# Two layers of cached-attention decode: one record of each round loaded in five pieces by rows, where it was one load of 128 rows

## The chip, the cores and the metric

The kernel runs on one core of a Trainium2 chip. The metric is the device time of one execution in microseconds. Before the change it is 730.65 us, the median of three runs (729.78 to 731.41).

## The reference, cut to what matters

A decode step for a batch of 4, one new position each, width 640. Two blocks are applied twice, with the same weights and the same cache both times: sliding-block attention over the last 1024 cached positions of 32 heads, and an MLP with a relu.

```python
x = A_x                                              # (4, 1, 640)
for _ in range(2):
    x = x + attention(layernorm(x))
    x = x + mlp(layernorm(x))

def attention(x):                                    # 32 heads of 128, no sharing of heads
    q = heads(x @ wq)                                # wq (640, 4096)
    k = k_cache[:, :, Sk - W:, :]                    # (4, 32, 1024, 128), W = 1024
    v = v_cache[:, :, Sk - W:, :]
    p = softmax(einsum("bhqd,bhkd->bhqk", q, k) * 128 ** -0.5)
    return join(einsum("bhqk,bhkd->bhqd", p, v)) @ wo   # wo (4096, 640)

def mlp(x):
    return maximum(x @ w1, 0) @ w2                   # w1 (640, 1728), w2 (1728, 640)
```

All of it is float32. The keys and values of one head for four batch rows are 4 MB, so over 32 heads and two rounds some 300 MB come from HBM.

## The kernel before, in words

**Records.** The host packs, for each head, everything that its attention needs into one record: an array of 128 rows and `REC` = 9472 columns (line 41), with the head's part of `wq`, the keys, the values and its part of `wo` side by side (`WQ`, `K`, `V`, `WO`, line 40). A row of a record is 37,888 bytes, lies in one partition, and is contiguous in HBM.

**Rounds.** A round is one attention block and one MLP. Round 0 goes through heads 0 to 31. Round 1 starts with the last five heads, 27 to 31, whose records are still in SBUF from round 0, and then takes heads 0 to 26 (`order`, line 126). So round 1 loads 27 records where round 0 loads 32.

**Buffers.** Five slots hold one record each (`NS`, line 45, and `slot`, line 108), and a ring of `RING` columns holds `w1` and `w2` in round 0 and takes the first records of round 1. `home` (line 129) says which slot a head's record goes to.

**The list of loads.** The kernel writes out all loads in order before it computes anything: `items` is a list, `load` (line 138) appends to it, `piece` (line 141) appends a range of columns of one record, `ending` (line 144) cuts the last three records of a round into seven column pieces (and, in round 0, three more for `wo`). Lines 154 to 165 write round 0's list: the first record in two pieces, then one load of all columns for each head of `hs[1:-3]`, the ending, five loads of `w1`, six of `w2`. Lines 168 to 189 write round 1's: ten loads that bring two records into the ring and freed slots, eight half records, one load of all columns for each head of `new[6:-3]`, the ending, four loads of `w1`, four of `w2`. That is 51 loads in each round.

**Issue.** `pump` (line 191) issues loads from the head of that list on SP's queue as long as the columns that they fill aren't live; each entry becomes one `dma_start` over all 128 partitions (line 197). `done` (line 212) frees columns when their last reader has been written out, and calls `pump`. Waits on semaphores are put in by the framework: SP waits for the readers of what a load overwrites, and TensorE waits for the loads whose columns it reads. `InOrder` (line 63) keeps the instructions of TensorE, VectorE, ScalarE and SP each in the order in which the program writes them; through it every instruction carries line 77 in the profile.

**The work on one record** (lines 373 to 394): `query` multiplies the normalized input with the record's part of `wq`, `query_T` transposes the result, `scores` makes 16 matmuls over the keys, `exponentials` runs on ScalarE, `weights_T` transposes the weights, `values` makes 64 matmuls over the values, `output_T` and `project` add the head's share to an accumulator in PSUM. The query of the next record is written ahead of the values of this one. After the last record of a round come `center` and `mlp`. The `busy` matmuls (line 229) between them write to a place that nothing reads.

All matmuls of a record read all 128 partitions of the columns concerned.

Of the kernel before, what the change touches and what calls it, by code (L numbers as in the profile page):

```python
# [31 lines left out]
P = 128  # L32
# [8 lines left out]
REC = 2 * D + 8 * W  # L41
# [13 lines left out]
W1_SLOT = [[0, 1], [2], [3], [4]]  # L55
W2_SLOT = [22, 20, 8, 4]
LATE = 3


IDENT, MEAN, NCON = 0, 128, 256  # L60
# [24 lines left out]
def decode_kernel(ctx: ExitStack, tc: tile.TileContext, xf, cst, rec, w1, w2, out):  # L85
    nc = tc.nc
    pe, dve, act, sp = (InOrder(tc, e) for e in (nc.tensor, nc.vector, nc.scalar, nc.sync))
# [12 lines left out]
    on = sb.tile([P, DH], F32, name="on")  # L100
    oTs = sb.tile([P, LATE, B], F32, name="oTs")
    qs = sb.tile([P, DH], F32, name="qs")
# [26 lines left out]
    def home(h, r):  # L129

        return h % NS if not r or h >= LAST else (h - 6 + LAST) % NS

    items = []
    at = {}
    live = []
    buffers = dict(enumerate(slot)) | {"ring": ring}

    def load(key, src, lo, hi, buf, col):
        items.append((key, src, lo, hi, buf, col))

    def piece(r, h, lo, hi, buf=None, col=None):
        load(("rec", r, h), rec[h], lo, hi, home(h, r) if buf is None else buf, lo if col is None else col)

    def ending(r, hs, late):
        a, b, c = hs[-3:]
        end = WO if late else REC
        for h, lo, hi in ((a, 0, V), (b, 0, V), (a, V, end), (c, 0, V), (b, V, end), (c, V, V + VH), (c, V + VH, end)):
            piece(r, h, lo, hi)
        if late:
            for h in hs[-3:]:  # L150
                piece(r, h, WO, REC)


    hs = order[0]
    piece(0, hs[0], 0, V)
    piece(0, hs[0], V, REC)
    for h in hs[1:-3]:
        piece(0, h, 0, REC)
    ending(0, hs, True)
    for k, col in enumerate(W1_RING):  # L160
        load(("w1", 0), w1, k * FF, k * FF + FF, "ring", col)
    n = 0
    for size, col in W2_RING:
        load(("w2", 0), w2, n * FD, (n + size) * FD, "ring", col)
        n += size


    hs = order[1]
# [10 lines left out]
        piece(1, new[i], 0, V, *((old[i], 0) if i < 5 else ("ring", 0)))  # L179
        piece(1, new[i], V, REC, old[i - 1], V)  # L180
    for h in new[6:-3]:
        piece(1, h, 0, REC)
    ending(1, hs, False)
    for blocks in W1_SLOT:
        load(("w1", 1), w1, blocks[0] * FF, (blocks[-1] + 1) * FF, home(LAST + 1, 0), blocks[0] * FF)
# [5 lines left out]
    def pump():  # L191

        while items:
            key, src, lo, hi, buf, col = items[0]
            if any(b == buf and x < col + hi - lo and col < y for b, x, y in live):
                return
            sp.dma_start(buffers[buf][:, col:col + hi - lo], src[:, lo:hi])
            live.append((buf, col, col + hi - lo))
            at.setdefault(key, []).append((lo, hi, buf, col))
            items.pop(0)  # L200
# [11 lines left out]
    def done(key, lo, hi):  # L212

        if key[0] == "rec" and key[1] == 0 and key[2] >= LAST:
            return
        for x, y, buf, col in pieces(key):
            a, b = col + max(lo, x) - x, col + min(hi, y) - x
            if a < b:
                rest = []
                for bb, u, v in live:  # L220
                    if bb != buf or v <= a or b <= u:
                        rest.append((bb, u, v))
                    else:
                        rest += [(bb, p, q) for p, q in ((u, a), (b, v)) if p < q]
                live[:] = rest
        pump()
# [6 lines left out]
    def center(fill):  # L233

        x = acc[:, :FD]
        dve.tensor_reduce(sums, x, op=OP.add, axis=AX.X)
        if fill:
            busy(256)
        pe.matmul(misc[:, 0:1], mean_of, sums, start=True, stop=True)
        if fill:  # L240
            busy(512)
            busy(256)
        dve.tensor_scalar(xc, x, misc[:, 0:1], None, op0=OP.subtract)
        dve.transpose(xT, xc)
        act.activation(square, xc, AF.Square, accum_out=squares)
        dve.tensor_copy(x_sb, x)
# [113 lines left out]


    pump()
    residual()
    for r in range(2):
        hs = order[r]
        late = LATE if r == 0 else 1
        center(r > 0)
# [78 lines left out]
```

## Time and profile before

| | before |
|---|---|
| median of 3 runs | 730.65 us (729.78 to 731.41) |
| the profiled execution, own time | 731.21 us |
| its span, first to last instruction | 729.4 us |
| mean granted TensorE clock | 0.854 |
| HBM read | 304.04 MB, 417 GB/s over the span |

How to read what follows. The page names engines PE (TensorE's matmuls), PEld (its weight loads), DVE (VectorE), ACT (ScalarE), POOL and SP; SPq is SP's DMA queue. Shares are of the span. In the strip of 40 slices a digit is a busy share in tenths, and "DMA" is the mean over the core's 16 DMA engines. A group line gives engine, operation, tiles, count, busy time and mean length of one, and behind the bar the idle time of that engine just before, with what ended it. An issue line gives count, size and the median time from issue to landing. A line of the chain of waits gives start, length and what it was. A row of the table by stretches gives the stretch, its length, busy time and count for PE, PEld, DVE, ACT and POOL, the granted clock, the DMA engines' mean share, and GB/s.

### The profile page before, as it was taken

Reading aid. Unit: us, or ns where it says so; the run is one execution under the profiler, and the core shown is the slowest. Engines: PE = TensorE matmul, PEld = TensorE weight load, DVE = VectorE, ACT = ScalarE, POOL = GpSimd, SP = SyncE. Lnnn points to the kernel's source line nnn. Section 1 sums busy time; section 2 is a strip of 40 time slices with the busy share of each in tenths; the row PEclk is TensorE's granted clock in tenths of the full one; section 3 lists DMA queues with packets and bytes.
Section 4 is the critical chain, followed back from the end, with each engine's and each line's share of the span. In section 5 each row is a group of like instructions: output and inputs, shape, how many; then the busy total and the mean of one; then the engine's idle time right before and its main releaser. Section 6 shows DMA issues by size and latency. Waiting matters only on the chain.

```text
span 729.4 us, 15682 instructions
## 1 busy us (share of the span) xinstructions
PE 517.4 (71%) x7300; PEld 266.3 (37%) x7300; DVE 179.2 (25%) x541; ACT 90.3 (12%) x154; POOL 0.2 (0%) x4
## 2 busy tenths in 40 slices
PE   0766867568667485778789888675857766667876
PEld 0233433334334243334433555332433333333532
DVE  1212222122222122212312334212212222122420
ACT  0201011011010101101111111101101011010110
POOL 0000000000000000000000000000000000000000
PEclk9978787787788777878999999968878888787999
DMA  9999999999999999999999999999999999999994
GB/s 377 432 430 431 428 431 431 430 431 431 430 431 431 430 431 430 431 431 411 417 375 376 408 427 423 433 429 430 431 431 432 429 431 428 431 430 420 424 421 199
DMA packets 15185, 305.12 MB, mean 418 GB/s; under 512 B 1681, under 2 KB 2065, under 8 KB 5137
## 3 DMA queue, kind: packets, MB, share of 16 engines
q1 hardware_dynamic: 14832, 303.91, 98.0%
q8 instruction: 57, 0.93, 0.5%
q10 hardware_dynamic: 288, 0.21, 0.1%
q14 instruction: 8, 0.06, 0.0%
HBM read 304.04 MB, written 0.08 MB: 417 GB/s over the span
## 4 chain that ended last, share of the span: by engine, by line
DMA 76%; PE 20%; DVE 2%; issue 1%; ACT 0%; SPq 0%; DVEq 0%; ACTq 0%
DMA slot<-rec 71%; PE sc_ps L77 7%; PE o_ps L77 4%; PE pt_ps L77 4%; DMA slot<-w 3%; DMA ring<-w 2%; PE q_ps L77 2%; PE acc L77 2%; PE misc L77 2%; DVE on L77 1%; DVE small L77 1%; DVE oTs L77 0%; ACT prob L77 0%; DVE qs L77 0%; SPq L77 0%
## 5 line engine op out<-in xcount | busy, mean ns | idle before, releaser
L77 PE MATMUL sc_ps<-slot,qT 128*1 128x512 f32 x992 | 152.8, 745 | 1.6 <-DVE qT L77 0.9
L77 PE MATMUL q_ps<-slot,xT 128*4 128x128 f32 x620 | 49.8, 333 | 133.1 <-DMA slot<-rec 132.3
L77 ACT ACTIVATE prob<-sc_ps,small 128x1024 f32<-128x1024 f32 x64 | 71.3, 1114 | 566.0 <-DVE small L77 557.2
L77 PE MATMUL o_ps<-slot,pT 128*1 128x128 f32 x4056 | 122.4, 273 | 5.2 <-DMA slot<-rec 4.3
L77 PEld LDWEIGHTS o_ps<-slot,pT 128*1 128x1 f32 x4056 | 99.3, 84 | 63.5 <-issue 46.8
L77 DVE TENSOR_REDUCE small<-sc_ps 128x1 f32<-128x1024 f32 x64 | 78.3, 1224 | 149.6 <-PE sc_ps L77 149.6
L77 PE MATMUL pt_ps<-con,prob 128*128 128x128 f32 x518 | 113.2, 360 | 0.0
L77 PEld LDWEIGHTS pt_ps<-con,prob 128*128 128x128 f32 x518 | 81.8, 185 | 23.2 <-issue 22.2
L77 PEld LDWEIGHTS q_ps<-slot,xT 128*4 128x4 f32 x620 | 21.4, 89 | 155.5 <-DMA slot<-rec 148.6
L77 DVE TENSOR_SCALAR qs<-q_ps,small 128x128 f32<-128x128 f32 x64 | 22.4, 350 | 209.9 <-PE q_ps L77 209.7
L77 PEld LDWEIGHTS sc_ps<-slot,qT 128*1 128x1 f32 x992 | 21.6, 92 | 82.0 <-issue 76.4
L77 PE MATMUL misc<-con,on 128*128 128x128 f32 x64 | 21.0, 328 | 30.5 <-DVE on L77 30.5
L77 PE MATMUL acc<-slot,oTs 128*4 128x160 f32 x512 | 29.1, 299 | 15.7 <-DVE oTs L77 15.5
L77 DVE COPY pT<-pt_ps 128x16 f32<-128x16 f32 x128 | 22.1, 174 | 62.5 <-PE pt_ps L77 62.5
L77 DVE TENSOR_SCALAR on<-o_ps,small 128x128 f32<-128x128 f32 x64 | 22.4, 350 | 35.0 <-PE o_ps L77 35.0
L77 PEld LDWEIGHTS misc<-con,on 128*128 128x128 f32 x64 | 8.9, 139 | 49.3 <-DVE on L77 49.3
L77 PE MATMUL misc<-con,qs 128*128 128x128 f32 x64 | 24.6, 385 | 2.3 <-DVE qs L77 2.1
L77 PE MATMUL sc_ps<-slot,con 128*1 128x512 f32 (+1 forms) x50 | 20.8, 506 | 0.0
L77 PEld LDWEIGHTS acc<-slot,oTs 128*4 128x4 f32 x512 | 7.2, 84 | 27.8 <-DVE oTs L77 27.7
L77 DVE COPY oTs<-misc 128x4 f32<-128x4 f32 x64 | 10.4, 162 | 27.0 <-PE misc L77 27.0
L77 PEld LDWEIGHTS misc<-con,qs 128*128 128x128 f32 x64 | 12.0, 187 | 6.5 <-ACT small L77 2.2
L77 ACT ACTIVATION_READ_ACCUMULATOR prob<-sc_ps,small 128x1 f32 x64 | 12.3, 193 | 0.0
(45 smaller groups left out, 97.7 us busy)
## 6 DMA issues: line engine op xcount, KB each, us to landing
slot<-rec SPq DMA_DIRECT2D x46, 4736.0 KB, 36.6
slot<-rec SPq DMA_DIRECT2D x17, 2368.0 KB, 24.3
slot<-rec SPq DMA_DIRECT2D x5, 1024.0 KB, 34.6
ring<-w SPq DMA_DIRECT2D x5, 864.0 KB, 13.9
slot<-rec SPq DMA_DIRECT2D x2, 2048.0 KB, 43.3
slot<-rec SPq DMA_DIRECT2D x3, 1344.0 KB, 11.0
slot<-w SPq DMA_DIRECT2D x3, 864.0 KB, 32.7
ring<-rec SPq DMA_DIRECT2D x1, 2368.0 KB, 18.7
```

The lines of the kernel that those rows point to most:

```text
L77: r = build(*args, **kwargs)
```

## The change

`load` and `piece` get one more argument, a list of row ranges, which stands in each entry of `items`; `pump` issues one `dma_start` for each row range, all of the same columns. The list is `EVEN`, one range of all 128 rows, for every entry but two: the record of `hs[20]` in each round, head 20 in round 0 and head 15 in round 1 (`hs` is `order[1]` there), is loaded by the five ranges of `UNEVEN`, 96 rows and four times 8 rows. The same bytes go to the same places, in the same place of the list.

```diff
+EVEN = [(0, P)]
+UNEVEN = [(0, 96), (96, 104), (104, 112), (112, 120), (120, P)]
+SHIFTED = 20
...
-    def load(key, src, lo, hi, buf, col):
-        items.append((key, src, lo, hi, buf, col))
+    def load(key, src, lo, hi, buf, col, rows=EVEN):
+        items.append((key, src, lo, hi, buf, col, rows))
 
-    def piece(r, h, lo, hi, buf=None, col=None):
-        load(("rec", r, h), rec[h], lo, hi, home(h, r) if buf is None else buf, lo if col is None else col)
+    def piece(r, h, lo, hi, buf=None, col=None, rows=EVEN):
+        load(("rec", r, h), rec[h], lo, hi, home(h, r) if buf is None else buf, lo if col is None else col, rows)
...
     for h in hs[1:-3]:
-        piece(0, h, 0, REC)
+        piece(0, h, 0, REC, rows=UNEVEN if h == hs[SHIFTED] else EVEN)
...
     for h in new[6:-3]:
-        piece(1, h, 0, REC)
+        piece(1, h, 0, REC, rows=UNEVEN if h == hs[SHIFTED] else EVEN)
...
-            key, src, lo, hi, buf, col = items[0]
+            key, src, lo, hi, buf, col, rows = items[0]
...
-            sp.dma_start(buffers[buf][:, col:col + hi - lo], src[:, lo:hi])
+            for a, b in rows:
+                sp.dma_start(buffers[buf][a:b, col:col + hi - lo], src[a:b, lo:hi])
```

## The prediction, made before the changed kernel was run

> **What bounds the kernel now.** I read the page first (busy shares, the DMA strip, the chain that ended last), then the queue's own waits, the chain in order of time, and last the stretches at the end of each round in steps of 1 us.
>
> ```profile
> span 729.4 us, 15682 instructions
> PE 517.4 (71%) x7300; PEld 266.3 (37%) x7300; DVE 179.2 (25%) x541; ACT 90.3 (12%) x154; POOL 0.2 (0%) x4
> DMA  9999999999999999999999999999999999999994
> DMA packets 15185, 305.12 MB, mean 418 GB/s; under 512 B 1681, under 2 KB 2065, under 8 KB 5137
> q1 hardware_dynamic: 14832, 303.91, 98.0%
> q8 instruction: 57, 0.93, 0.5%
> DMA 76%; PE 20%; DVE 2%; issue 1%; ACT 0%; SPq 0%; DVEq 0%; ACTq 0%
> L77 PE MATMUL q_ps<-slot,xT 128*4 128x128 f32 x620 | 49.8, 333 | 133.1 <-DMA slot<-rec 132.3
> slot<-rec SPq DMA_DIRECT2D x46, 4736.0 KB, 36.6
> ```
>
> The loads bound it: SP's queue q1 keeps the 16 DMA engines moving 98% of the span, and TensorE's idle time is almost all before the query matmuls, 132.3 us of waiting for a record. A load lands 36.6 us after its issue, so some three loads always stand in line. The chain of waits gives the pace:
>
> ```profile
> 483.77 37.87 DMA slot<-rec
> 521.68 0.60 PE q_ps L77 x10
> ...
> 528.64 37.90 DMA slot<-rec
> 566.58 0.60 PE q_ps L77 x10
> ...
> 575.15 36.30 DMA slot<-rec
> ```
>
> Landings at 521.6 and 566.5 are 44.9 us and four records apart: 11.2 us a record. TensorE takes 575.15 - 566.58 = 8.6 us for one.
>
> The queue's packets tell how a load is split. The kernel's lists hold 51 loads for each round, and with the store of the result SP issues 103; 14832 / 103 = 144 = 128 + 16, and 103 x 16 = 1648 accounts for nearly all of the 1681 packets under 512 B. So a row of a load is one packet, moved whole by one engine, and each of the 16 engines closes its share with one small packet. In full stretches the DMA share is 1.00:
>
> ```profile
> 600.00:650.00 50.00, 33.31 (x455) 18.39 (x459) 11.60 (x36) 4.82 (x8) 0.00 (x0) 0.80 1.00 428
> 715.00:716.00 1.00, 0.93 (x9) 0.19 (x9) 0.00 (x0) 0.00 (x0) 0.00 (x0) 1.00 0.98 406
> 716.00:717.00 1.00, 0.92 (x6) 0.22 (x2) 0.00 (x0) 0.64 (x2) 0.00 (x0) 1.00 0.80 330
> 717.00:718.00 1.00, 1.00 (x6) 0.40 (x5) 0.17 (x1) 0.51 (x2) 0.00 (x0) 1.00 0.65 271
> 718.00:719.00 1.00, 0.14 (x2) 0.00 (x0) 0.21 (x1) 0.00 (x0) 0.00 (x0) 1.00 0.55 232
> 719.00:720.00 1.00, 0.43 (x16) 0.38 (x20) 0.00 (x0) 0.00 (x0) 0.00 (x0) 1.00 0.48 200
> 720.00:721.00 1.00, 1.00 (x38) 0.81 (x28) 0.00 (x0) 0.00 (x0) 0.00 (x0) 1.00 0.47 195
> 721.00:722.00 1.00, 0.37 (x8) 0.02 (x2) 0.00 (x0) 0.00 (x0) 0.00 (x0) 1.00 0.43 172
> 722.00:723.00 1.00, 0.00 (x0) 0.00 (x0) 0.00 (x0) 0.00 (x0) 0.00 (x0) 1.00 0.21 82
> 725.00:726.00 1.00, 0.93 (x20) 0.33 (x18) 0.00 (x0) 0.00 (x0) 0.00 (x0) 1.00 0.01 5
> ```
>
> The last two columns are DMA share and GB/s. They show the one thing on which this change can act: the engines don't finish together. The last loads are in every engine's line before 716, yet engines begin to stop at about 716.8, half of them have stopped by 719 (0.48 x 16 = 7.7 still move), and the last stops at 725.7. That is a slow half, up to 8.9 us behind the first engine, and a fast half, spread over 719.0 - 716.8 = 2.2 us. The instruction packets of q8 (57 of them, 0.93 MB, in the engines' lines beside the rows) are what can set engines apart; no row says which engines carry them. When others stop, an engine gets no faster (195 / 0.47 / 16 = 25.9 GB/s against 428 / 16 = 26.8), so the limit lies with each engine or with the rows that it writes, not with the memory. The same dip stands at the end of round one:
>
> ```profile
> 370.00:371.00 1.00, 0.97 (x12) 0.40 (x4) 0.32 (x1) 0.00 (x0) 0.00 (x0) 1.00 0.99 408
> 371.00:372.00 1.00, 1.00 (x5) 0.29 (x5) 0.77 (x3) 0.32 (x2) 0.00 (x0) 1.00 0.78 307
> 372.00:373.00 1.00, 1.00 (x11) 0.30 (x9) 0.17 (x1) 0.98 (x3) 0.00 (x0) 1.00 0.58 228
> 373.00:374.00 1.00, 1.00 (x7) 0.52 (x4) 0.00 (x0) 0.66 (x2) 0.00 (x0) 1.00 0.60 249
> ```
>
> Half the engines wait there too, for at least 3 us, so the slowest lags by 3 to 8.9 us; I take 6.
>
> **The change part by part.** *Removed:* one load of 128 rows in each round, 8 rows for each engine. A row is 4736 KB / 128 = 37,888 B; at 26.8 GB/s it takes 1.41 us, and 8 take 11.3, which agrees with the 11.2 us pace.
>
> *Added, the 96 rows:* 6 for each of 16 engines, 8.4 us.
>
> *Added, four loads of 8 rows:* as a row is one packet on one engine, such a load can use at most eight engines, so the eight that take part carry 6 + 4 = 10 rows of this record and the others 6. No load of fewer than 128 rows is in the trace, so one load's price is bounded from both sides. If only the engine limits, it is one row, 1.41 us. If the rows written limit, 8 rows get their 8/128 of 428 GB/s, 26.8 GB/s, and take 11.3 us. A price below 1.41 is excluded, since an engine gets no faster alone. The eight rows of one load are adjacent, and in the rows shown no eight rows ever receive more than one engine's rate; that leans away from the low end. But eight adjacent rows need not hang on one limit only, which leans away from the high one. I take the middle, 6.3 us. The eight engines then need 8.4 + 4 x 6.3 = 33.6 us for the record, 33.6 - 11.3 = 22.3 more than before (bounds 2.8 and 42.3).
>
> Here a rule of the Trainium skill bears on the price: SBUF — State Buffer, "Door 1: The DMA port swizzle", says that a transfer's rate follows how many of 16 ports its rows reach, about 27.2 GB/s a port, four adjacent rows on one port. By it eight rows reach two ports, and 303 KB take an estimated 5.6 us: 19.5 us more for the record instead of 22.3, and about 764 us in the end by the sum below. It speaks against the change; the rows above fit it as well as they fit a limit in the engine.
>
> *Where the delay goes.* The four small loads stand in line on the eight engines ahead of the next three records, so the record lands some 22 us late, TensorE starves there once, and its slot is released as late. The other engines don't run dry: they have the three records behind it, 33 us, in line. The eight engines never catch up inside a round (share 1.00), so every later record comes as late, at the old pace, up to the end of the round, where the last landing sets the MLP. Round two repeats it: its loads into the ring wait for TensorE to consume what lies there, so the first delay passes on whole.
>
> *The sum.* At the end of round two, if the eight are the fast half, the last landing moves from 725.7 to 719.0 + 22.3 = 741.3: +15.6. If they are the slow half: +22.3. In round one, with a fast half spread over 2 us and a lag of 6: +22.3 - 4 = +18.3, or +22.3. Together +33.9 or +44.6. No row tells which half takes the rows; I take the middle, +39.3.
>
> *Issues and waits:*
>
> ```profile
> L77 SPq DMA_DIRECT2D slot<-rec x76: 327/328/653, 1.2 to 667.3; - x76
> SPq L77 <- PE acc L77: 482.7, 53, 21.4
> SPq L77 <- DMA slot<-rec: 84.1, 21, 6.5
> ```
>
> Eight more issues of 328 ns are 2.6 us of SP, which already stands 482.7 us waiting for slots; they are hidden by the 36.6 us line of loads, and cost 1.3 us a round if that line were gone. SP also waits at times for an earlier load (up to 6.5 us); four more loads in flight can bring such waits for the next records' issues, with only later loads queued behind them, and 6.5 us is well inside the line. TensorE's first query matmul waits for five loads in place of one: nothing beside its present wait of some 3 us a record. I cost these at 0.
>
> The profiled execution took 731.21 us, 0.56 over the median of 730.65, and its span is 729.4. 731.21 + 39.3 = 770.5; against the median, 770 us.
>
> **The rivals.**
>
> *The engine alone limits, and the fast half takes the rows: faster.* A small load costs 1.41 us, the eight engines get 2.8 us more in each round and the others 2.8 less. In round two the slow half ends 8.9 - 2.8 = 6.1 us after the first stop and the fast half at 2.2 + 2.8 = 5.0: -2.8. In round one, 6 - 2.8 = 3.2 against 2 + 2.8 = 4.8, a gain of 1.2, or none if the fast half spreads over 3.2: I take -0.5. Sum -3.3, 727.3 us. For it: the two halves in the windows, and that two rows move just half the gap. Against it: it needs eight engines to write eight adjacent rows at 16 times the rate that eight rows get now over a whole load. It decides where a small load takes under (4 + 6.7 + 2 x 2.8) / 8 = 2.0 us; above that the loss outweighs. The Trainium skill has a rule for who takes them (DMA: Bandwidth & Descriptors, "Why a DMA increments its semaphore by 16 and not by 1"): eight rows run on the eight lowest-numbered engines. Nothing in the trace shows whether these are the fast ones.
>
> *The engine alone limits, and the slow half takes the rows.* +2.8 us in each round: 736.3 us. For it: the halves are as likely this way round.
>
> *The change does nothing to the engines' shares:* rows stay with the engine that writes them in a whole load, so each still moves 8. 730.7 us. For it: the limit may lie with the rows. Against it: a split by count gives 6 rows of 96 to each engine.
>
> **How the numbers follow.** Forecast (crowded rows) 0.55; faster rival 0.28; slow half at engine rate 0.08; nothing 0.09. The forecast's own range is 747 to 786: a small load of 4.1 us with the fast half gives 8.8 us less a round (+16.3, 747), one of 7.6 with the slow half 5.2 more (+55, 786). The high bound of 11.3 us would give over 800, which I hold at 0.05. To hold 8 in 10 the range reaches from the faster rival, 727, to 782; about 0.1 lies above. What this measurement can tell from no change is about 0.2%, 1.5 us. Faster: the second case and a little, 0.29. Same: most of the fourth, 0.08. Slower: the rest, 0.63.
>
> **What would show it.** The packets of q1: with eight engines on each small load the count rises by 2 x 32 to 14896 (four times eight more closing packets a round); with two engines each, by 16. The median landing of the 8-row loads and the wait of TensorE before the split record: near 25 us where the rows crowd, near 3 at engine rate. In the last stretches: a plateau of half the engines lasting some 20 us for the forecast; the first stop later and the last stop earlier for the faster rival. The forecast is wrong if the small loads take under 2 us each, or if the late engines catch up before the round ends.

## The result, and the profile after

The changed kernel takes 784.71 us (782.86 to 785.66, four runs) against 730.21 us for the kernel before in the same job: a ratio of 1.0744, 95% interval 1.0715 to 1.0773. It is 54.5 us slower. The forecast was slower, 770, with a range that ended at 782: the way was right, the size too small.

The page of the changed kernel, its heads and the strip of bandwidth:

```profile
span 782.9 us, 15696 instructions
DMA  9999999999999999999989999999999999999994
GB/s 383 433 432 431 431 431 432 433 424 429 428 355 171 225 431 431 431 428 419 409 327 360 420 428 434 430 429 429 431 431 225 125 376 433 431 431 419 427 420 197
q1 hardware_dynamic: 14896, 303.91, 97.7%
DMA 66%; PE 23%; another core or an unknown queue 8%; DVE 2%; issue 1%; SPq 0%; ACT 0%; DVEq 0%; ACTq 0%
L81 PE MATMUL q_ps<-slot,xT 128*4 128x128 f32 x620 | 51.5, 341 | 186.6 <-DMA slot<-rec 185.8
```

The loss stands in two places of the GB/s strip, slices 12 to 14 and 31 to 33, one in each round; elsewhere the rate is about what it was. The DMA share doesn't show it: the engines count as busy while a packet crawls. TensorE's wait for records rose from 132.3 to 185.8 us, by 53.5, which is the growth of the span (782.9 - 729.4). The 14896 packets are the number that the prediction gave for eight engines on each small load. The same matmul, the last projection of round 0, stands at these places of the chain of waits, in the changed kernel first and then in the kernel before:

```profile
397.46 0.46 PE acc L81 x8
```

```profile
369.88 0.45 PE acc L77 x8
```

So round 0 loses 27.6 us and round 1 the other 25.9 of the span's 53.5. The first place in steps of 4 us, in the changed kernel (the last two columns are DMA share and GB/s):

```profile
228.00:232.00 4.00, 1.30 (x29) 0.44 (x17) 0.72 (x4) 1.21 (x2) 0.00 (x0) 1.00 1.10 237
232.00:236.00 4.00, 1.12 (x11) 0.55 (x12) 0.07 (x1) 0.00 (x0) 0.00 (x0) 0.66 1.00 218
236.00:240.00 4.00, 4.00 (x21) 2.00 (x25) 0.81 (x4) 0.00 (x0) 0.00 (x0) 0.50 1.11 227
240.00:244.00 4.00, 3.26 (x81) 1.75 (x73) 1.81 (x4) 1.21 (x2) 0.00 (x0) 0.99 0.83 170
244.00:248.00 4.00, 0.15 (x7) 0.00 (x0) 0.00 (x0) 0.00 (x0) 0.00 (x0) 0.87 1.24 156
248.00:252.00 4.00, 0.00 (x0) 0.00 (x0) 0.00 (x0) 0.00 (x0) 0.00 (x0) 0.50 1.11 142
252.00:256.00 4.00, 0.00 (x0) 0.00 (x0) 0.00 (x0) 0.00 (x0) 0.00 (x0) 0.50 0.99 142
256.00:260.00 4.00, 0.00 (x0) 0.00 (x0) 0.00 (x0) 0.00 (x0) 0.00 (x0) 0.50 1.07 152
260.00:264.00 4.00, 0.00 (x0) 0.00 (x0) 0.00 (x0) 0.00 (x0) 0.00 (x0) 0.50 0.84 142
264.00:268.00 4.00, 0.00 (x0) 0.00 (x0) 0.00 (x0) 0.00 (x0) 0.00 (x0) 0.50 0.78 180
268.00:272.00 4.00, 0.00 (x0) 0.00 (x0) 0.00 (x0) 0.00 (x0) 0.00 (x0) 0.50 0.91 341
272.00:276.00 4.00, 3.78 (x23) 2.29 (x27) 0.88 (x4) 0.00 (x0) 0.00 (x0) 0.50 1.01 436
```

There are two steps. From 228 to 240 the rate is about half of 430, and from 244 to 264 it is a third, 142 to 156. Against 430 GB/s the eleven rows up to 272 lose 4 us x (430 - rate) / 430 each, 24.4 us together, most of the round's 27.6. The first figure behind the comma is TensorE's busy time: it has next to nothing to do from 244 to 272, since the split record is late. In the chain that wait has no name; it seems that the view doesn't recognize the completions of loads that fewer than 16 engines carry:

```profile
244.15 27.83 another core or an unknown queue
272.22 1.01 PE q_ps L81 x10
```

What ended it can be read from the completions in the trace, one for each engine that takes part in a load (16 for a load of 128 or 96 rows, eight for a small load). The first and the last completion of each load, in us:

| load | changed kernel, first and last | before, first and last |
|---|---|---|
| the record ahead, 128 rows | 227.99, 234.83 | 228.12, 231.55 |
| the split record: 96 rows (before: 128) | 244.98, 257.24 | 239.34, 242.78 |
| its four small loads, one after another | 250.08, 259.94; 254.19, 264.14; 258.90, 268.34; 262.88, 271.98 | |
| the record behind, 128 rows | 272.22, 282.95 | 250.57, 255.24 |

The last small load is complete at 271.98, where TensorE's wait ends. The prediction had that wait near 25 us if the rows crowd, and it is 27.8. The engine that is first has its part of the 96 rows at 244.98. Up to there no engine is on a small load, and the low rate is due to the 96 rows. Then the leading engines go on to the small loads while the last is on its 96 rows up to 257.24, so the second step mixes the two.

### The profile page after: what moved, and what is told of

Its sections match the earlier page's. It is cut to its first block, busy times and chain, and to the rows that moved or that the text cites. A ratio compares the mean times of both kernels' runs of the same rounds, so it can differ in the third digit from the quotient of the medians.

```text
span 782.9 us, 15696 instructions
## 1 busy us (share of the span) xinstructions
PE 518.4 (66%) x7300; PEld 269.8 (34%) x7300; DVE 179.2 (23%) x541; ACT 90.3 (12%) x154; POOL 0.2 (0%) x4
## 3 DMA queue, kind: packets, MB, share of 16 engines
q1 hardware_dynamic: 14896, 303.91, 97.7%
## 4 chain that ended last, share of the span: by engine, by line
DMA 66%; PE 23%; another core or an unknown queue 8%; DVE 2%; issue 1%; SPq 0%; ACT 0%; DVEq 0%; ACTq 0%
DMA slot<-rec 61%; PE sc_ps L81 7%; PE o_ps L81 5%; PE pt_ps L81 5%; DMA slot<-w 3%; PE q_ps L81 2%; DMA ring<-w 2%; PE acc L81 2%; PE misc L81 2%; DVE on L81 1%; DVE oTs L81 0%; DVE small L81 0%; SPq L81 0%; ACT prob L81 0%
## 5 line engine op out<-in xcount | busy, mean ns | idle before, releaser
L81 PE MATMUL q_ps<-slot,xT 128*4 128x128 f32 x620 | 51.5, 341 | 186.6 <-DMA slot<-rec 185.8
L81 PE MATMUL sc_ps<-slot,qT 128*1 128x512 f32 x992 | 150.0, 733 | 1.6 <-DVE qT L81 0.9
L81 PE MATMUL pt_ps<-con,prob 128*128 128x128 f32 x518 | 115.7, 367 | 0.0
L81 PEld LDWEIGHTS pt_ps<-con,prob 128*128 128x128 f32 x518 | 83.8, 189 | 24.1 <-issue 23.2
L81 PEld LDWEIGHTS acc<-slot,oTs 128*4 128x4 f32 x512 | 7.2, 84 | 27.8 <-DVE oTs L81 27.6
```

The source lines that it names most:

```text
L81: r = build(*args, **kwargs)
```

## The experiments

Fifteen kernels, each the changed kernel with the edit shown, unless said otherwise. Two kinds of theory ran through all of them: that adjacent rows crowd where they are written, in groups of partitions that share the rate of one engine (theory A), and that something else about the loads costs the time: their number (B), the unequal shares of the engines (C), or adjacent rows on the side that is read (D). The times are against the kernel before in the same job; one run each, except for `c5` (ten) and `shift` (five), so that differences of a microsecond or two between the others mean little. The changed kernel is +54.5. A comment behind a line of the edits names the kernel that has it.

| kernel | the split record of each round | difference, us |
|---|---|---|
| c5 | five loads by columns, all 128 rows | +0.9 |
| h64 | 2 x 64 adjacent rows | +33.1 |
| h32 | 4 x 32 adjacent rows | +32.5 |
| r96_32 | 96, then 32 adjacent rows | +31.6 |
| st32 | 4 x 32 rows, step 4 | +0.7 |
| h32_src | 4 x 32: partitions adjacent, HBM rows step 4 | +32.6 |
| st32_src | 4 x 32: partitions step 4, HBM rows adjacent | +0.2 |
| src_st | as changed, small loads read HBM rows with step 4 | +56.6 |
| st4 | 96, then 4 x 8 rows, step 4 | +42.6 |
| low | rows 32 on in one load of 96, then 4 x 8 adjacent of rows 0 to 31 | +42.2 |
| low_st | the same, small loads with step 4 | +32.3 |
| shift | 3 x 32 with step 4, 4 x 8 with step 4 | +14.5 |
| q23 | as changed, on the first 2,176 columns only | +11.1 |
| r0 | as changed, in round 0 only | +28.7 |
| probe | none; the very last load of `w2` as 112, 8 and 8 rows | +1.7 |

**The number of loads.** `c5` makes as many loads as the change, by columns.

```diff
+COLS = [(0, 1896), (1896, 3792), (3792, 5688), (5688, 7584), (7584, REC)]
...
-            for a, b in rows:
-                sp.dma_start(buffers[buf][a:b, col:col + hi - lo], src[a:b, lo:hi])
+            for a, b in cols or [(lo, hi)]:
+                sp.dma_start(buffers[buf][:, col + a - lo:col + b - lo], src[:, a:b])
```

> The record of hs[20] in five loads by columns, each over all 128 rows, in place of five loads by rows: as many loads, issues and semaphores as in the changed kernel. Theory A (rows crowd: a group of adjacent rows takes no more than one engine's rate, 27 GB/s, and only a load over all 128 rows keeps 16 engines out of each other's way): 0, within 1.5 us of before. Rival B (the number of loads, their issues and SP's waits for earlier loads cost the time): +20 to +54 us.

731.25 against 730.35 us, ratio 1.001 (1.0001 to 1.002). The number of loads, the issues and the waits of SP cost nothing that counts here.

**Equal shares for all engines.** `r96_32` and `h64` take the unequal shares away and leave the split by rows.

```diff
-UNEVEN = [(0, 96), (96, 104), (104, 112), (112, 120), (120, P)]
+UNEVEN = [(0, 96), (96, P)]       # r96_32
+UNEVEN = [(0, 64), (64, P)]       # h64
```

> 96 rows, then 32 rows in one load instead of four of 8: 6 and 2 rows for each of 16 engines, so no engine carries more than another. Theory A: the 96 rows take 17 us in place of 8.4 (2.8 us a row, as in the changed kernel's trace), the 32 rows, two engines to four adjacent rows, 5.6 in place of 2.8: +11 us a round, +22 in all. Rival C (only the eight engines with ten rows cost the time, each row at the engine's own rate or at a price of the small loads): 0 within 1.5 us.

> Two loads of 64 adjacent rows, 4 rows for each engine in each. Theory A in its stricter form (the groups that share a rate are four adjacent rows together with the four that lie 32 rows off, so 64 adjacent rows hold eight groups): each load at half rate, 11.3 us, +11.3 us a round, +22 in all, with two engines on each group throughout. If the groups are eight adjacent rows the same 64 rows hold eight groups too: +22. Rival C (the engines' shares alone count): 0 within 1.5 us.

+31.6 and +33.1. That unequal shares alone cost is out: here each engine moves eight rows of the record and more than half of the loss is still there. Both theories missed the size, A by a third: it has the two loads at half rate, which gives +22.

**Rows of a small load spread out.** `st4` takes the last 32 rows with a step of 4.

```diff
+UNEVEN = [(0, 96, 1), (96, P, 4), (97, P, 4), (98, P, 4), (99, P, 4)]
-                sp.dma_start(buffers[buf][a:b, col:col + hi - lo], src[a:b, lo:hi])
+                sp.dma_start(buffers[buf][a:b:n, col:col + hi - lo], src[a:b:n, lo:hi])
```

> The 96 rows as in the changed kernel, and the four loads of 8 rows taken with a step of 4 (rows 96, 100, ... 124, then 97, 101, ...), so that the eight rows of one load lie in eight groups of four. Same count of loads, same engines, same rows per engine. Theory A: each small load shares its groups only with the engines that write them anyway, 2.8 us in place of about 5: the record costs some 8 to 10 us less a round than in the changed kernel, so +54 falls to +30 to +40. Rival B or C (count of loads, or unequal shares of the engines at a fixed price): +54 as before.

+42.6, a little above what A said: 12 us of the loss are the adjacency inside the small loads. The completions agree: on the engine that is first a small load takes 3.1 us, where it takes 4.5 in the changed kernel. The 96 rows, which `r96_32` and `st4` share, take that engine 17.1 us in both.

**Read or written.** `src_st` leaves the partitions of the change as they are and spreads the rows that the small loads read; the host orders the last rows of two extra copies of the records.

```diff
+UNEVEN = [(0, 96, 0, 96, 1), (96, 104, 96, P, 4), (104, 112, 97, P, 4), (112, 120, 98, P, 4), (120, P, 99, P, 4)]
-                sp.dma_start(buffers[buf][a:b, col:col + hi - lo], src[a:b, lo:hi])
+                sp.dma_start(buffers[buf][a:b, col:col + hi - lo], src[c:d:n, lo:hi])
```

> As the changed kernel, the four small loads writing 8 adjacent partitions each, but reading from HBM rows that lie four rows apart (the host puts the last 32 rows of a copy of these two records in another order). Theory A (the rows written crowd): +54 as the changed kernel, within 2 us. Rival D (adjacent rows read from one place of HBM crowd): it falls to what the loads with step 4 on both sides gave, +42.6.

+56.6, 2 us above the changed kernel: no gain from reading elsewhere.

**The other end of the partitions.** `low` and `low_st` put the small loads on rows 0 to 31.

```diff
+UNEVEN = [(32, P), (0, 8), (8, 16), (16, 24), (24, 32)]                            # low
+UNEVEN = [(32, P, 1), (0, 32, 4), (1, 32, 4), (2, 32, 4), (3, 32, 4)]              # low_st
```

> The record as 96 rows from row 32 on, and rows 0 to 31 in four loads of 8 adjacent rows. If the small loads run on the eight engines that write rows 0 to 63 of a whole load (theory A with the lowest eight engines), four engines share a group of four rows while that group's own engine is one of the eight: 5.6 us a small load, four of them 22.5. Sum near the changed kernel: +45 to +58. Rival C: the same as the changed kernel, +54.

> The same with the rows 0 to 31 taken with a step of 4: the eight rows of a small load lie in eight groups, and if the small loads run on the eight engines that write those groups anyway, each row at most meets what the 96 rows left: 1.4 us a small load in place of 5.6. Theory A: 16.7 us a round less than with adjacent rows, some 33 us less in all, +15 to +28. If the small loads ran on the other eight engines, each group would be shared by two: 2.8 us, some 22 us less than with adjacent rows. Rival C (ten rows on eight engines at a fixed price): the same as with adjacent rows.

+42.2 and +32.3: both outside what A said, from opposite sides. The step helps here too, but by 10 us and not by 33. In `low_st` a row takes 2.9 us in the median between 228 and 250, while the 96 rows are under way, and 1.4 again from 254 on, as the last of them lands (254.9): most of its loss is that of the 96 rows. So A had the weights wrong: it put most of the loss into the small loads. Why small loads cost less on rows 0 to 31 than on 96 to 127, adjacent or not, is taken up under `shift`.

**Four loads of 32.** `h32` has them adjacent, `st32` with a step of 4.

```diff
+UNEVEN = [(0, 32), (32, 64), (64, 96), (96, P)]                                    # h32
+UNEVEN = [(0, P, 4), (1, P, 4), (2, P, 4), (3, P, 4)]                              # st32
```

> The record in four loads of 32 adjacent rows, two rows for each engine in each load. If a group that shares one engine's rate is four adjacent rows and the four that lie 32 rows off, 32 adjacent rows hold eight groups, two engines on each, half rate as with 64 adjacent rows: +33 as that kernel, within 8. If a group is eight adjacent rows, 32 rows hold four groups, quarter rate: 4 x 11.3 = 45 us a record in place of 11.3, +60 us or more in all. Rival C (only unequal shares of the engines cost): 0.

> The record in four loads of 32 rows taken with a step of 4, two rows for each engine in each load; each load's rows span all sixteen groups. If what counts is how many groups a load's rows reach: 0 to +3. If what counts is which groups the sixteen engines write at the same moment: engines e and e+4 of a half stand on one group in step, eight groups at a time: up to +33, less as far as the engines fall out of step.

+32.5 and +0.7. This is the sharpest pair: the same number of loads, of rows in a load, of rows for each engine, of bytes. While the split record loads, in `h32` first and then in `st32`:

```profile
228.00:232.00 4.00, 0.62 (x9) 0.11 (x8) 0.16 (x1) 0.22 (x2) 0.00 (x0) 0.85 0.94 208
236.00:240.00 4.00, 4.00 (x49) 2.34 (x51) 0.83 (x5) 0.00 (x0) 0.00 (x0) 0.79 0.96 208
248.00:252.00 4.00, 0.00 (x0) 0.00 (x0) 0.00 (x0) 0.00 (x0) 0.00 (x0) 0.50 0.85 180
256.00:260.00 4.00, 2.54 (x18) 1.99 (x19) 0.70 (x3) 0.00 (x0) 0.00 (x0) 0.50 0.90 369
```

```profile
228.00:232.00 4.00, 0.36 (x8) 0.24 (x9) 0.00 (x0) 0.00 (x0) 0.00 (x0) 0.61 0.97 417
236.00:240.00 4.00, 3.26 (x81) 1.85 (x77) 1.81 (x4) 1.21 (x2) 0.00 (x0) 1.00 1.06 449
244.00:248.00 4.00, 4.00 (x34) 2.40 (x37) 0.88 (x4) 0.00 (x0) 0.00 (x0) 0.75 1.01 436
```

About half the rate against the full rate. 32 adjacent rows are no slower than 64 (+32.5 and +33.1), which a group of eight adjacent rows would not allow. That engines which meet on one group would slow each other even with a step of 4 did not come about in `st32`.

**Which side, with the pair.** `h32_src` and `st32_src` take the two steps apart, with the host putting the rows of the two extra copies in the order that each needs.

```diff
+UNEVEN = [(slice(32 * j, 32 * j + 32), slice(j, P, 4)) for j in range(4)]          # h32_src: partitions, rows of HBM
+UNEVEN = [(slice(j, P, 4), slice(32 * j, 32 * j + 32)) for j in range(4)]          # st32_src
-                sp.dma_start(buffers[buf][a:b, col:col + hi - lo], src[a:b, lo:hi])
+                sp.dma_start(buffers[buf][to, col:col + hi - lo], src[of, lo:hi])
```

> Four loads of 32 adjacent partitions, each reading every fourth row of a copy of the record whose rows the host has put in the order that this needs. Theory A (the partitions written crowd): +32, as with 32 adjacent rows on both sides. Rival D (adjacent rows of HBM crowd): 0 to +2.

> Four loads to every fourth partition, each reading 32 adjacent rows of HBM. Theory A: 0 to +2, as with step 4 on both sides. Rival D: +32.

+32.6 and +0.2. The partitions that a load writes decide, the rows that it reads don't.

**By bytes, and by round.** `q23` splits 23% of the record's columns, `r0` splits in one round.

```diff
+            piece(0, h, 0, K + 1536, rows=UNEVEN)        # q23, and the same in round 1
+            piece(0, h, K + 1536, REC)
...
-        piece(1, h, 0, REC, rows=UNEVEN if h == hs[SHIFTED] else EVEN)
+        piece(1, h, 0, REC)                              # r0
```

> Only the first 2,176 of the record's 9,472 columns are loaded by 96 and four times 8 rows, the rest in one load of 128 rows; 23% of the bytes, and one load more than in the changed kernel. Theory A (each row that crowds costs its time): 0.23 x 54.5 = +12.5, within 4. Rival B (a price for each small load whatever its size): +54.

> The changed kernel with the split in round 0 alone. If the late engines never catch up inside a round and each round loses its own: half of +54, +26 to +29, and the end of round 1 as in the kernel before. If the loss of round 0 is partly made up in round 1: under +24.

+11.1, a fifth of 54.5 for 23% of the bytes: the price goes with bytes, not with loads. +28.7, half of it: each round loses its own, and nothing of it is made up later.

**Who carries the small loads.** `probe` is the kernel before, with its very last load cut so that the completions tell when the eight engines of a small load are through.

```diff
-        load(("w2", 1), w2, n * FD, (n + size) * FD, home(LAST + 2, 0), n * FD)
+        load(("w2", 1), w2, n * FD, (n + size) * FD, home(LAST + 2, 0), n * FD,
+             [(0, 112), (112, 120), (120, P)] if size == 4 else [(0, P)])
```

> The kernel before with nothing changed but its last load (w2, 2,560 bytes a row): 112 rows, then two loads of 8 rows, which show when the eight engines that small loads run on reach the end of their line. If these are the fast half: the two loads of 8 rows land 3 to 9 us before the load of 112 rows that stands ahead of them. If they are the slow half: after it. Time within 1.5 us of before.

The time is 1.7 us over before, a little more than was expected. The completions in the trace, one for each engine, in us:

```
112 rows   716.8 716.8 717.2 717.3 717.4 718.0 718.9 719.9   721.8 722.2 722.5 722.8 723.7 723.8 724.1 726.7
8 rows     717.0 717.0 717.5 717.5 718.2 720.0               722.1 723.9
8 rows     717.2 717.2 717.7 717.7 718.4 720.2               722.3 724.1
```

Six of the eight engines belong to the fast half and two to the slow one; the slowest, at 726.7, is not among them. Neither of the two expectations, all fast or all slow.

**The shift itself, with little to crowd.** `shift` gives ten rows to those eight engines and six to the others, as the change does, out of loads with a step of 4.

```diff
+UNEVEN = [(0, P, 4), (1, P, 4), (2, P, 4), (3, 32, 4), (35, 64, 4), (67, 96, 4), (99, P, 4)]
```

> Rows 0, 4, 8, ..., then 1, 5, ..., then 2, 6, ... in three loads of 32, and rows 3, 7, ... in four loads of 8 with a step of 4 in place of the fourth load of 32: 10 rows on the eight engines of small loads and 6 on the others, as in the changed kernel, with little to crowd. If the engines' shares were what bounds the end of a round (the faster rival): -1 to -3.3. If a row goes no faster than its group of partitions lets it, whichever engine carries it (theory A): the two small loads that go to partitions 64 to 127 share the groups of the other engines, 2.8 us a row in place of 1.4, and nothing is gained: 0 to +8.

745.04 against 730.52 us, ratio 1.0204 (1.019 to 1.0218): +14.5, more than either theory said. In its trace:

```profile
232.00:236.00 4.00, 4.00 (x27) 2.17 (x22) 0.87 (x4) 0.00 (x0) 0.00 (x0) 0.50 0.97 417
236.00:240.00 4.00, 3.71 (x76) 1.70 (x68) 1.51 (x3) 0.63 (x1) 0.00 (x0) 0.81 1.30 440
240.00:244.00 4.00, 0.78 (x9) 0.25 (x9) 0.30 (x2) 0.58 (x2) 0.00 (x0) 1.00 0.83 171
244.00:248.00 4.00, 0.00 (x0) 0.00 (x0) 0.00 (x0) 0.00 (x0) 0.00 (x0) 0.54 1.25 275
248.00:252.00 4.00, 0.04 (x4) 0.08 (x8) 0.00 (x0) 0.00 (x0) 0.00 (x0) 0.50 0.67 218
252.00:256.00 4.00, 4.00 (x27) 2.35 (x31) 0.87 (x4) 0.00 (x0) 0.00 (x0) 0.50 0.99 426
```

The three loads of 32 pass at the full rate. By the completions the engine that is first then takes 1.41, 1.41, 3.1 and 2.9 us for its four small loads. The first two write partitions 0 to 63, the last two 64 to 127: the two that A named, at about the price that it gave. From 241 to 248 all rows take 2.6 to 3.0 us, whatever engine carries them, and the engine that is last needs 11.2 us for its four small rows (240.54 to 251.71), where the two rows of a whole load in their place take 2.8. These 8.4 us cover the 7.3 that each round loses.

Small loads to the upper partitions are dearer in the other kernels too, each time on the engine that is first: 4.5 us in the changed kernel against 3.2 in `low`, and 3.1 in `st4` against 2.4 in `low_st`. It fits A's idea that there they meet the other eight engines; as no trace shows which engine writes which partitions, it isn't shown. Ten rows for some engines and six for others didn't pay here either, but two of the four small loads were slow: a split with strided small loads to partitions 0 to 63 alone is not among the runs.

## Why the prediction was right in the way and wrong in the size

*What bounds the kernel* held: loads set the pace, and the whole loss is TensorE's longer wait for records.

*The 96 rows* are the term that was mis-sized. The prediction took "6 for each of 16 engines, 8.4 us", at the engine's own rate, and gave no bounds, though the same doubt that it raised for eight adjacent rows holds for 96. In the trace the engine that is first takes 244.98 - 227.99 = 17.0 us for its six rows, 2.8 us a row in place of 1.41, and 16.9 to 17.1 us in `r96_32`, `st4`, `low` and `low_st`, whatever follows them. `r96_32`, where 32 adjacent rows follow and no small load, loses 31.6 us, more than half of 54.5.

*The four small loads* were put too high, not too low. The prediction took 6.3 us each, the middle of 1.41 and 11.3; the engine that is first took (262.88 - 244.98) / 4 = 4.5 us for each, and 5.1 in round 1. The rule of the Trainium skill that the prediction set beside them (SBUF — State Buffer, "Door 1: The DMA port swizzle") gives an estimated 5.6, more than was measured. Its example, that 64 rows are no faster than 32, is what `h64` and `h32` show: eight ports at its 27.2 GB/s are an estimated 218, and `h32` ran at 208 in two of the rows above. What the rule doesn't give is half rate for 96 rows: by its map they reach all sixteen ports.

With 17.0 and 4.5 the record would take the prediction's eight engines 17.0 + 4 x 4.5 = 35.0 us in place of 33.6. The two errors nearly cancel, which is luck, and the sum comes to 39.3 + 2 x 1.4 = 42.1, still 12 us short of 54.5. So a second step failed.

*Where the delay goes* is that step. The prediction had eight engines 22 us late and the others at full rate, a fast half that could absorb part of the delay (it took the middle, 39.3, where 44.6 has nothing absorbed), and a plateau of half the engines for some 20 us at the end. The trace has all engines slow together while the rows crowd. The 16 completions of the very last load lie between 716.81 and 725.67 in the kernel before and between 767.48 and 779.17 in the changed one: even the engine that is first is 50.7 us late, and nothing is absorbed. There is no plateau:

```profile
770.00:772.00 2.00, 1.92 (x7) 0.39 (x5) 0.17 (x1) 1.09 (x3) 0.00 (x0) 1.00 0.82 335
772.00:774.00 2.00, 1.58 (x32) 1.11 (x35) 0.21 (x1) 0.06 (x1) 0.00 (x0) 1.00 0.33 133
774.00:776.00 2.00, 0.88 (x24) 0.41 (x13) 0.00 (x0) 0.00 (x0) 0.00 (x0) 1.00 0.15 60
```

The share falls from 0.82 to 0.15 within 4 us, as the engines finish one after another. The last completions of the table above give the delay in round 0: the record ahead lands 3.3 us late already, the split record takes 37.2 us behind it in place of 11.2 and is 29.2 late, and the record behind is 27.7 late, where the prediction had 22.3. That the loss isn't made up later, and that each round pays its own, was right (`r0`).

*Issues and waits*, costed at 0, cost 0 (`c5`).

*The rivals.* The faster one needed small loads under 2.0 us; they took 4.5 to 5.1. The "16 times the rate" that the prediction held against it should be 8: 11.3 / 1.41. Its premise about who is slow was mostly right (`probe`), yet `shift`, the nearest to it, loses 14.5 us, with small loads of 2.2 us in the mean. The slow half at engine rate needed 1.41 us for each. Rows that stay with their engine: the packet count rules it out for the small loads, 14896 and not 14848.

## What to carry to other kernels

A split by rows isn't free though bytes, loads and shares of engines stay equal: here only loads that spread over the whole range of 128 partitions and over all 16 engines were free (five loads by columns cost 0.9 us for two records, four loads of every fourth partition 0.7, four of 32 adjacent ones 32.5). If a record must come in pieces, cut it by columns. When a price is bounded from both sides for one half of an edit, ask whether the other half escapes the same doubt, and read GB/s beside the DMA share: a share of 1.00 says nothing of the rate.

## What the runs showed of the hardware that was not expected

While crowded partitions were written, the rows of all engines slowed down. In the changed kernel the last of the 96 rows lands at 257.24 us. Then eight engines are on the small loads and the other eight on the record behind, and each of the 18 rows that began between 257.3 and 262 took 3.7 to 4.4 us, where a row takes 1.41 in the kernel before; none was spared. In `h32` a row took 1.41 us before the split record and 2.7 to 3.1 from 230 to 254. The record ahead, which isn't split, is slowed at its end: it lands at 234.60 in `h32`, against 231.55 in the kernel before. Why, and why small loads to partitions 64 to 127 cost more, stays open, and no run shows how a load of fewer than 128 rows is dealt out to the engines row by row. The rule of the Trainium skill named above (SBUF — State Buffer, "Door 1: The DMA port swizzle") says which partitions share a port, which fits `h32`, `h64` and `st32`; it says nothing of engines that write elsewhere.
